# LayerNorm rows, y and late dO staged differently in the first part of a fused forward and backward block

## The chip, the core and the metric

The kernel runs on one core of one Trainium2 chip. The metric is the device time in microseconds (us); the time before is the median of five runs. The trace and the page that are quoted come from one profiled execution, whose own time stands in the table below.

## What is computed

A block of attention times a gate, forward and backward, for S = 2048 rows, D = 512, 32 heads of 16, and a hidden width F = 1792:

```python
xn = _layernorm(x)                       # eps 1e-5, no weights
s  = softmax(q k^T / 4) v  @ wo          # q, k, v = xn @ wqkv, 32 heads
y  = _layernorm(xn)                      # a second LayerNorm on the first
m  = gelu(y @ w1 + b1) @ w2 + b2
g  = silu(m)
out = x + s * g
```

The kernel returns `out` and the gradients with respect to x, wqkv, wo, w1, b1, w2 and b2 for a given grad_out. All tensors are bfloat16. The rows of x are cut into 16 tiles of 128 rows, and four tiles make a group.

## The kernel before

The program has three parts, one after the other, each written out by hand in the order of issue. Every engine takes its instructions in program order; a wait of one instruction holds all those behind it on its engine. DMAs are issued in order on SP (`nc.sync`), ACT (`nc.scalar`) or POOL (`nc.gpsimd`).

**First part, `phase_pre`.** It is the one that the change touches, apart from one line of the last part.

*k, v, q (L67 to L174).* x is loaded in four groups (L76, SP), wqkv and w1 by ACT (L78, L79). `ln1(g)` takes statistics of a group on DVE (`stats`: L86, L87, then a root on ACT, L89, a reciprocal and a product on DVE, L90, L91) and normalises: group 0 on DVE with transposes on PE (L96, L113, L114), the other groups on ACT (L102) with a DMA transpose on SP into xnT (L117). `ln2(g)` does the same once more on xn in place and sends it, transposed, to yT (L121 to L124). `hooks` says after which tile each is emitted. xn has three buffers for four groups, so that of group 0 is used again for group 3, after the transpose that reads it. For each tile PE makes k, v, q with 12 matmuls into three PSUM banks (L144, six banks in turn), ACT copies them (L149 to L151) into NSall (k and v; two buffers for four groups) and NQ, POOL squares k and q (L155, `sq`, three buffers), and DVE sums the squares by head (L130) one tile later. At the end of a group, SP stores NSall and NQ (L167, L168). After tile 5, SP issues the loads of b1, b2, w2 and the transposed wo (L160 to L163). Then the largest k norm is taken over all partitions on POOL (L174); `row_bound` uses it after h1(1).

*h1, m and gate (L182 to L304).* `h1(sc)` makes 14 matmul groups of four (L195) from yT and w1; DVE adds the bias into h1row (L198, eight buffers), ACT takes gelu (L199), SP stores h1row (L200). `m_step(t)` for each tile emits, in this order, a transpose of dso for tile t-2, `proj` for t-5 (dso times wo: L251, copy on ACT L253, store of NATQd_s on SP L255 after every fourth), `gate` for t-1 (DVE L218, L220, POOL L224 to L226; gB has four buffers), `slope_out` for t-3 (DVE L230, store of GB_s on SP L231) and the 14 matmuls of `m_mm` (L209). The order is h1(0), h1(1), the four tiles of group 0, h1(2), those of group 1, h1(3), and so on. The last four tiles of `proj`, from LATE = 12 on, use `late_sb`, which lies where w1 was and which attention will use as the third `eg` buffer. It holds a second copy of the transposed wo (L288, a DMA transpose on SP from DRAM), the late dsoT, and the late dO (`late_sb[:, 4:8]`). These steps are emitted by `rest` (L292) between the first steps of attention.

**Second part, `attention_core`.** 1024 steps for 16 pairs of heads, 16 steps to a block and 4 blocks to a pair. Each step has score matmuls (L786, L798) and exponentials on ACT (L812, L820), a product on DVE (L830) and accumulating matmuls; after every fourth step SP transposes what was made from `eg` to `tg` (L841). The three `eg` buffers change every four steps. Before a pair, POOL loads its operands from DRAM (L324 to L328), arranges them in `Pad`, and SP transposes them into KVT and QDT (L336, L345). For pair 0 the last 12 tiles of QDT come after the start: POOL's load of NATQd at step 7 (it reads NATQd_s), the arrangement at step 9, the transpose at step 11. Step 16 is the first to need them. The second set of KVT and QDT belongs to pair 1.

**Last part, `phase3`.** Weight and input gradients. `y_all` is computed again from xn_all on ACT (L545) between the matmuls of dw2.

Of the kernel before, what the change touches and what calls it, by code (L numbers as in the profile page):

```python
# [16 lines left out]
LATE = 12  # L17
# [20 lines left out]
def phase_pre(tc, k, A_x, A_wqkv, A_wo, B_w1, B_b1, B_w2, B_b2, grad_out):  # L38
# [4 lines left out]
    with ExitStack() as c1:  # L43
# [23 lines left out]
        with ExitStack() as c0:  # L67
# [3 lines left out]
            NSall = p0.tile([128, 2, NPAIR, 4, 2, NATW], bf16, name="NSall")  # L71
# [10 lines left out]
            def stats(g, src, rstd_all, nmr_all):  # L82
                s6 = wk0.tile([128, 4, nc.vector.BN_STATS_DIM], f32, name="ln_st")
                mv = wk0.tile([128, 4, nc.vector.BN_AGGR_DIM], f32, name="ln_mv")
                for i in range(4):
                    nc.vector.bn_stats(out=s6[:, i, :], in_=src[:, i, :])  # L86
                    nc.vector.bn_aggr(out=mv[:, i, :], in_=s6[:, i, :])  # L87
                rs = rstd_all[:, 4 * g:4 * g + 4]
                nc.scalar.activation(out=rs, in_=mv[:, :, 1], func=ACT.Sqrt, bias=k.eps_t[:], scale=1.0)  # L89
                nc.vector.reciprocal(out=rs, in_=rs)  # L90
                nc.vector.scalar_tensor_tensor(out=nmr_all[:, 4 * g:4 * g + 4], in0=mv[:, :, 0], scalar=-1.0, in1=rs, op0=ALU.mult, op1=ALU.mult)  # L91
                return mv, rs

            def norm(dst, src, mv, rs):
                for i in range(4):
                    nc.vector.tensor_scalar(out=dst[:, i, :], in0=src[:, i, :], scalar1=mv[:, i, 0:1], scalar2=rs[:, i:i + 1],  # L96
                                            op0=ALU.subtract, op1=ALU.mult)

            def norm_act(dst, src, g, rstd_all, nmr_all):
                for i in range(4):  # L100
                    t = 4 * g + i
                    nc.scalar.activation(out=dst[:, i, :], in_=src[:, i, :], func=ACT.Identity, bias=nmr_all[:, t:t + 1], scale=rstd_all[:, t:t + 1])  # L102

            def ln1(g):
                src = x_all[:, 4 * g:4 * g + 4, :]
                mv, rs = stats(g, src, k.rstd1, k.nmr1)
                xn[g] = p0.tile([128, 4, D], bf16, name="xn", bufs=3)
                if g == 0:
                    norm(xn[g], src, mv, rs)
                    for i in range(4):  # L110
# [4 lines left out]
                else:  # L115
                    norm_act(xn[g], src, g, k.rstd1, k.nmr1)
                    nc.sync.dma_start_transpose(out=xnT[:, 4 * g:4 * g + 4].rearrange("c t m q -> c (t m) q"),  # L117
                                                in_=xn[g][:].rearrange("q t c -> q (t c)"))

            def ln2(g):  # L120
                mv, rs = stats(g, xn[g], k.rstd2, k.nmr2)  # L121
                norm_act(xn[g], xn[g], g, k.rstd2, k.nmr2)
# [8 lines left out]
            ln1(0)  # L131
            ln1(1)
            hooks = {1: lambda: ln1(2), 3: lambda: ln2(0), 5: lambda: ln1(3), 8: lambda: ln2(1), 11: lambda: ln2(2), 14: lambda: ln2(3)}
            for t in range(NT):
# [3 lines left out]
                ns = NSall[:, i4 % 2]  # L138
# [14 lines left out]
                for dst, v in ((kn2, kk), (qn2, qq)):  # L153
                    sq = wk0.tile([128, H, DH], f32, name="sq", bufs=3)
                    nc.gpsimd.tensor_tensor(out=sq[:].rearrange("p (a j) c -> p a j c", j=2), in0=v, in1=v, op=ALU.mult)  # L155
                    sqs[t].append((dst, sq))
                if t in hooks:
                    hooks[t]()
                if t == 5:
# [4 lines left out]
                if t >= 1:  # L164
                    reduce_of(t - 1)
                if t % 4 == 3:
                    nc.sync.dma_start(out=k.NAT_s[:, :, t - 3:t + 1, :].rearrange("a p t c -> p a t c"), in_=ns.rearrange("p a t j c -> p a t (j c)"))  # L167
                    nc.sync.dma_start(out=k.NATQq_s[:, :, t - 3:t + 1, :].rearrange("a p t c -> p a t c"), in_=NQ[:].rearrange("p a t j c -> p a t (j c)"))  # L168
            reduce_of(NT - 1)
            nc.vector.tensor_copy(out=b1c[:], in_=b1_bf[:])  # L170
            nc.vector.tensor_copy(out=b2bc[:], in_=b2_bf[:])
            kmaxrun = wk0.tile([128, H], f32, name="kmaxrun", bufs=1)
# [9 lines left out]
        with ExitStack() as c0:  # L182
# [62 lines left out]
            def proj(t, pd=None):  # L245
# [6 lines left out]
                nd = ND[(t // 4) % 2] if t < LATE else late_sb[:, 4:8].rearrange("p b m q -> p (b m q)").rearrange("p (a b c) -> p a b c", a=NPAIR, b=4)  # L252
                nc.scalar.copy(out=nd[:, :, t % 4, :].rearrange("p a (j c) -> p a j c", j=2), in_=pd[:].rearrange("p (a j c) -> p a j c", a=NPAIR, j=2))  # L253
                if t % 4 == 3:
                    nc.sync.dma_start(out=k.NATQd_s[:, :, t - 3:t + 1, :].rearrange("a p t c -> p a t c"), in_=nd[:] if t < LATE else nd)  # L255
# [22 lines left out]
            for sc in range(4):  # L278
# [7 lines left out]
                if sc == 1:  # L286
                    late_sb = eg_as(2, [128, 16, IC, 128], "late_sb")
                    nc.sync.dma_start_transpose(out=late_sb[:, 0:4].rearrange("p b m q -> p b (m q)"), in_=A_wo)  # L288
            store_h(3)
            nc.scalar.activation(out=kmax2[:, 0:1], in_=k.eps_t[:], func=ACT.Exp)  # L290
# [5 lines left out]
            for t in range(NT - 5, LATE):  # L296
                proj(t)

            def rest(psum):
                proj(LATE, psum([128, 512], f32))  # L300
# [3 lines left out]
                for t in range(LATE + 1, NT):  # L304
                    proj(t, psum([128, 512], f32))
# [69 lines left out]
def phase3(ctx, tc, k, A_x, A_wqkv, A_wo, B_w1, B_w2, grad_out, out_0, out_1, out_2, out_3, out_4, out_5, out_6, out_7):  # L375
# [5 lines left out]
    with ExitStack() as c1:  # L381
# [23 lines left out]
        with ExitStack() as c2:  # L405
# [128 lines left out]
            for i in range(7):  # L534
# [8 lines left out]
                if i < 6:  # L543
                    for t in range(3 * i, min(3 * i + 3, NT)):
                        nc.scalar.activation(out=y_all[:, t, :], in_=xn_all[:, t, :], func=ACT.Identity, bias=k.nmr2[:, t:t + 1], scale=k.rstd2[:, t:t + 1])  # L545
# [121 lines left out]
def attention_core(ctx, tc, k, rest_of_pre, npairs=16, nqc=4):  # L667
# [330 lines left out]
    rest = rest_of_pre(lambda shape, dt: ps_z.tile(shape, dt, name="Z0", tag="z"))  # L998
# [56 lines left out]
def full_kernel(ctx, tc, A_x, A_wqkv, A_wo, B_x, B_w1, B_b1, B_w2, B_b2, grad_out,  # L1055
# [13 lines left out]
    k.nmr2 = persist.tile([128, NT], f32, name="nmr2")  # L1069
    k.ones_bf = persist.tile([128, 1], bf16, name="ones_bf")  # L1070
    nc.vector.memset(k.ones_bf[:], 1.0)
    persist.tile([128, 64], mybir.dt.uint8, name="pad_to_256")
# [90 lines left out]
```

## Time and profile before

| | |
|---|---|
| median of five runs | 2344.5 us (2332.8 to 2386.55) |
| the profiled execution: time | 2358.49 us |
| its span, first to last instruction | 2356.3 us |
| busy: PE, DVE, ACT, POOL | 2201.1, 1798.2, 1854.8, 1193.4 us |
| first part, up to the start of m (0 to 94.88 us): PE busy | 72.47 us |
| h1(2), h1(3), m and gate (94.88 to 188.09 us): PE busy | 88.78 us |
| start of attention (188.09 to 234.97 us): PE busy, mean clock | 38.74 us, 0.75 |
| rest of attention (234.97 to 1978 us): PE busy, mean clock | 1675.27 us, 0.95 |
| last part (1978 to 2356.3 us): PE busy | 325.84 us |

The page gives, for each engine, busy time and idle time, and for idle time what ended it. "A <- B: 7.4, 4, 2.3" in the list of waits says that A waited 7.4 us in total for B, in four places, 2.3 us in the longest. In the timeline a line is start, duration, engine (SPq, ACTq, POOLq are the queues that issue DMAs), source line, operation, output and inputs, and in brackets the idle time before it and what ended it. The clock is the share of full speed that TensorE was granted.

### The profile page before, as it was taken

How to read it: one execution, taken by the hardware profiler on the slowest of the kernel's cores; microseconds unless marked ns; L12 is line 12 of the kernel's file. 1: busy time of each engine (PE TensorE's matmuls, PEld its weight loads, DVE VectorE, ACT ScalarE, POOL GpSimd, SP SyncE). 2: the span in 40 equal slices, each digit the busy share in tenths (PEclk: the TensorE clock that was granted, in tenths of full speed). 3: DMA queues.
4: the chain of work that ended last, by engine and by line, in shares of the span. 5: the costliest groups of instructions: out<-in, count | busy, mean ns of one | idle time of the engine just before them, and what ended most of it. 6: DMA issues, size and time to landing. Idle time of an engine off the chain costs nothing.

```text
span 2356.3 us, 47583 instructions
## 1 busy us (share of the span) xinstructions
PE 2201.1 (93%) x18320; PEld 731.6 (31%) x18320; DVE 1798.2 (76%) x2994; ACT 1854.8 (79%) x2159; POOL 1193.4 (51%) x1956
## 2 busy tenths in 40 slices
PE   6998999999999999999999999999999998689997
PEld 3442222222222222222222222222222222234456
DVE  6766987898899799969987998988898893204641
ACT  6645988999999799979998999998998994221231
POOL 4355564656474647555665656574756554200020
PEclk9997997999999799969998999998998998999999
DMA  8778999999999999999999999999999998998546
GB/s 228 221 221 215 228 239 205 243 249 246 240 240 250 194 242 246 246 189 239 245 253 214 246 244 237 243 250 216 244 239 227 245 233 228 209 231 251 160 80 130
DMA packets 1763637, 530.42 MB, mean 225 GB/s; under 512 B 1684417, under 2 KB 1749074, under 8 KB 1763410
## 3 DMA queue, kind: packets, MB, share of 16 engines
q1 hardware_dynamic: 1719890, 468.25, 97.8%
q10 hardware_dynamic: 31200, 31.73, 4.7%
q0 software_dynamic: 12320, 27.41, 3.9%
q8 instruction: 143, 2.34, 0.4%
q14 instruction: 84, 0.69, 0.1%
HBM read 47.98 MB, written 58.33 MB: 45 GB/s over the span
## 4 chain that ended last, share of the span: by engine, by line
PE 50%; ACT 21%; DMA 12%; POOL 6%; issue 4%; DVE 2%; ACTq 0%; SPq 0%; POOLq 0%; DVEq 0%
ACT eg L812 9%; ACT e L820 9%; PE d L798 9%; PE s L786 8%; PE X L856 8%; DMA tg<-eg 7%; PE X L868 4%; PE Z L964 3%; PE X L880 2%; PE ps_dhg L581 2%; PE ps_dy L596 2%; PE ps_m L209 2%; DMA xt<-in_A_x_dram 1%; DMA hgc<-HGT_s 1%; PE ps_dw L539 1%
## 5 line engine op out<-in xcount | busy, mean ns | idle before, releaser
L830 DVE TENSOR_TENSOR eg<-d,eg 128x512 bf16<-128x512 f32 x2048 | 1349.7, 687 | 207.8 <-PE d L798 76.6
L812 ACT ACTIVATE eg<-s 128x1024 bf16<-128x1024 f32 x1024 | 1042.3, 1035 | 84.5 <-PE d L798 63.2
L798 PE MATMUL d<-QDT,KVT 32*128 32x512 bf16 x2048 | 816.6, 399 | 0.3 <-DVE eg L830 0.2
L820 ACT ACTIVATE e<-t 128x1024 bf16<-128x1024 f32 x640 | 663.6, 1037 | 53.6 <-PE t L772 52.2
L786 PE MATMUL s<-QDT,KVT 32*128 32x512 bf16 x2048 | 414.3, 399 | 47.2 <-ACT eg L812 41.8
L868 PE MATMUL X<-eg,NAT 128*32 128x512 bf16 x2048 | 419.3, 407 | 0.0
L856 PE MATMUL X<-eg,Lc 128*32 128x512 bf16 x2048 | 418.8, 406 | 0.0
L880 PE MATMUL X<-eg,NAT 128*17 128x512 bf16 x2048 | 412.4, 400 | 0.0
L798 PEld LDWEIGHTS <-KVT 32*128 32x128 bf16 x2048 | 186.4, 91 | 353.5 <-issue 353.4
L952 PE MATMUL Z<-e,W 128*32 128x512 bf16 x1280 | 261.5, 404 | 20.0 <-POOL W L919 19.0
L772 PE MATMUL t<-KVT,QDT 32*128 32x512 bf16 x1280 | 259.8, 400 | 1.8 <-ACT eg L812 1.5
L913 POOL TENSOR_TENSOR W<-NATQd,rL 128x128 bf16<-128x128 bf16 x64 | 25.8, 404 | 380.5 <-DVE rL L897 380.5
L964 PE MATMUL Z<-tg,W 128*32 128x512 bf16 x2048 | 213.0, 398 | 0.0
L786 PEld LDWEIGHTS <-KVT 32*128 32x128 bf16 x2048 | 116.9, 91 | 306.1 <-issue 304.4
L856 PEld LDWEIGHTS <-Lc 128*32 128x32 bf16 x2048 | 99.0, 93 | 288.8 <-issue 288.8
L952 PE MATMUL Z<-tg,W 128*32 128x512 bf16 x768 | 157.4, 407 | 0.0
L868 PEld LDWEIGHTS <-NAT 128*32 128x32 bf16 x2048 | 99.2, 94 | 170.5 <-issue 170.5
L719 POOL TENSOR_TENSOR bg_v<-bg_t 128x512 f32<-128x512 f32 x56 | 57.9, 1034 | 180.8 <-ACT bg_t L734 180.4
L978 DVE TENSOR_TENSOR acc<-Z,acc 128x512 f32<-128x512 f32 x192 | 130.5, 680 | 14.2 <-PE Z L964 14.2
L372 POOL TENSOR_TENSOR dx<-lnb_prod,lnb_dy 128x512 bf16<-128x512 f32 x16 | 20.9, 1311 | 233.6 <-DMA dout<-in_grad_out_dram 210.1
L952 PEld LDWEIGHTS <-W 128*32 128x32 bf16 x2048 | 109.2, 93 | 48.7 <-POOL W L919 23.3
L880 PEld LDWEIGHTS <-NAT 128*17 128x17 bf16 x2048 | 93.0, 88 | 61.4 <-issue 61.4
(173 smaller groups left out, 2760.6 us busy)
## 6 DMA issues: line engine op xcount, KB each, us to landing
H1T_s<-h1row SPq DMA_DIRECT2D x56, 128.0 KB, 1.8
HGT_s<-hgT SPq DMA_DIRECT2D x4, 1792.0 KB, 7.8
bg_x<-H1T_s POOLq DMA_DIRECT2D x56, 128.0 KB, 5.3
GP_s<-bg_m POOLq DMA_DIRECT2D x56, 128.0 KB, 5.4
gp<-GP_s ACTq DMA_DIRECT2D x8, 896.0 KB, 6.9
DH1T_s<-dh1T SPq DMA_DIRECT2D x4, 1792.0 KB, 9.6
NAT_s<-NSall SPq DMA_DIRECT2D x4, 1056.0 KB, 6.4
NAT<-NAT_s POOLq DMA_DIRECT2D x16, 264.0 KB, 5.8
```

Of the source, the lines that this page charges most:

```text
L772: nc.tensor.matmul(t[:, hj, :], lhsT=op["QDT"][r:r + 32, q0:q0 + 128], rhs=op["KVT"][r:r + 32, kc * 512:(kc + 1) * 512], start=True, stop= ...
L786: nc.tensor.matmul(s[:, hj, :], lhsT=op["KVT"][r:r + 32, kb * 128:(kb + 1) * 128], rhs=op["QDT"][r:r + 32, qc * 512:(qc + 1) * 512], start ...
L798: nc.tensor.matmul(d[:], lhsT=op["KVT"][r:r + 32, kb * 128:(kb + 1) * 128], rhs=op["QDT"][r:r + 32, qc * 512:(qc + 1) * 512], start=True, ...
L812: nc.scalar.activation(out=cur["eg"][1][:, :, kb % 4, :, :].rearrange("k b h q -> k h b q"), in_=st_s.pop(g)[:].rearrange("k h (b q) -> k ...
L820: nc.scalar.activation(out=e[:], in_=st_t.pop(g)[:], func=ACT.Exp)
L830: nc.vector.tensor_tensor(out=gts[:, kb % 4, hj, :].rearrange("k (b q) -> k b q", b=4), in0=ds[hj][:].rearrange("k (b q) -> k b q", b=4), ...
L856: nc.tensor.matmul(X[64 + 32 * hj:96 + 32 * hj, :], lhsT=Lc[:], rhs=et[:, :, kb % 4, hj, :], start=(kb == 0), stop=False, skip_group_check ...
L868: nc.tensor.matmul(X[32 * hj:32 * hj + 32, :], lhsT=NATt[:, kb, hj, 1:33], rhs=et[:, :, kb % 4, hj, :], start=(kb == 0), stop=(kb == 15), ...
L880: nc.tensor.matmul(X[64 + 32 * hj:64 + 32 * hj + 17, :], lhsT=NATt[:, kb, hj, 0:17], rhs=gts[:, kb % 4, hj, :], start=False, stop=(kb == 1 ...
L952: nc.tensor.matmul(Z[32 * hj:32 * hj + 32, :], lhsT=blk[j]["W1"][:, qb, hj, :], rhs=ev[:, hj], start=(i == 0), stop=False, tile_position=( ...
L964: nc.tensor.matmul(Z[c:c + 32, :], lhsT=blk[j]["W2"][:, qb, hj, :], rhs=gv[:, :, hj, qb, :], start=(i == 1), stop=(i >= 2), tile_position= ...
L978: nc.vector.tensor_tensor(out=av, in0=Z[:], in1=av, op=ALU.add)
```

## The change

- Statistics and rows are two functions. `ln_stats` takes DVE statistics of x. `ln_rows` forms rstd1 and nmr1, and from the first variance also the variance of xn (variance times rstd1 squared), from which `ln_apply` makes rstd2 with a root and a reciprocal. There is no second set of statistics, and the mean of xn is taken as zero.
- `ln_apply` normalises and transposes as `ln1` did. y is xn times rstd2: group 0 on DVE after tile 5, groups 1 to 3 on POOL after the loop.
- The schedule: rows of group 1 and statistics of group 2 after tile 0, group 1 is normalised after tile 1, and so on as `hooks` says.
- NSall has three buffers, sq has five, and the sums of squares are taken two tiles later.
- b1, b2, w2 and the transposed wo are issued after tile 0.
- The second copy of wo is made by DVE from the first.
- Late dO is staged in the second operand set's QDT, and its store is issued by ACT.
- The small Exp that loads the table of exponentials is emitted after the last `proj` before attention.
- y_all in the last part has no bias; nmr2 is gone and the padding keeps the size.

```diff
-            NSall = p0.tile([128, 2, NPAIR, 4, 2, NATW], bf16, name="NSall")
+            NSall = p0.tile([128, 3, NPAIR, 4, 2, NATW], bf16, name="NSall")
...
+            def ln_stats(g):
                 s6 = wk0.tile([128, 4, nc.vector.BN_STATS_DIM], f32, name="ln_st")
+                mvs[g] = wk0.tile([128, 4, nc.vector.BN_AGGR_DIM], f32, name="ln_mv")
                 for i in range(4):
+                    nc.vector.bn_stats(out=s6[:, i, :], in_=x_all[:, 4 * g + i, :])
+                    nc.vector.bn_aggr(out=mvs[g][:, i, :], in_=s6[:, i, :])
+
+            def ln_rows(g):
+                mv = mvs.pop(g)
+                rs, rs2, nm = (t_[:, 4 * g:4 * g + 4] for t_ in (k.rstd1, k.rstd2, k.nmr1))
                 nc.scalar.activation(out=rs, in_=mv[:, :, 1], func=ACT.Sqrt, bias=k.eps_t[:], scale=1.0)
                 nc.vector.reciprocal(out=rs, in_=rs)
+                nc.vector.scalar_tensor_tensor(out=nm, in0=mv[:, :, 0], scalar=-1.0, in1=rs, op0=ALU.mult, op1=ALU.mult)
+                nc.vector.tensor_tensor(out=rs2, in0=mv[:, :, 1], in1=rs, op=ALU.mult)
+                nc.vector.tensor_tensor(out=rs2, in0=rs2, in1=rs, op=ALU.mult)
+                if g == 0:
+                    ln_apply(g, mv)
+
+            def ln_apply(g, mv=None):
+                rs, rs2, nm = (t_[:, 4 * g:4 * g + 4] for t_ in (k.rstd1, k.rstd2, k.nmr1))
+                xn[g] = p0.tile([128, 4, D], bf16, name="xn", bufs=3)
                 for i in range(4):
                     t = 4 * g + i
+                    if g == 0:
+                        nc.vector.tensor_scalar(out=xn[g][:, i, :], in0=x_all[:, t, :], scalar1=mv[:, i, 0:1], scalar2=rs[:, i:i + 1],
+                                                op0=ALU.subtract, op1=ALU.mult)
                         pt = psT.tile([128, IC, 128], bf16, name="tp_ps", tag="tp")
                         for b in range(IC):
                             nc.tensor.transpose(pt[:, b, :], xn[g][:, i, b * 128:(b + 1) * 128], k.ident_bf[:])
                         nc.scalar.copy(out=xnT[:, i, :, :], in_=pt[:])
+                    else:
+                        nc.scalar.activation(out=xn[g][:, i, :], in_=x_all[:, t, :], func=ACT.Identity, bias=nm[:, i:i + 1], scale=rs[:, i:i + 1])
+                if g > 0:
                     nc.sync.dma_start_transpose(out=xnT[:, 4 * g:4 * g + 4].rearrange("c t m q -> c (t m) q"),
                                                 in_=xn[g][:].rearrange("q t c -> q (t c)"))
+                nc.scalar.activation(out=rs2, in_=rs2, func=ACT.Sqrt, bias=k.eps_t[:], scale=1.0)
+                nc.vector.reciprocal(out=rs2, in_=rs2)
 
             def ln2(g):
-                mv, rs = stats(g, xn[g], k.rstd2, k.nmr2)
-                norm_act(xn[g], xn[g], g, k.rstd2, k.nmr2)
+                for i in range(4):
+                    rs2 = k.rstd2[:, 4 * g + i:4 * g + i + 1]
+                    (nc.vector if g == 0 else nc.gpsimd).tensor_scalar(out=xn[g][:, i, :], in0=xn[g][:, i, :], scalar1=rs2, scalar2=None, op0=ALU.mult)
                 nc.sync.dma_start_transpose(out=yT[:, 4 * g:4 * g + 4].rearrange("c t m q -> c (t m) q"),
                                             in_=xn[g][:].rearrange("q t c -> q (t c)"))
...
-            ln1(0)
-            ln1(1)
-            hooks = {1: lambda: ln1(2), 3: lambda: ln2(0), 5: lambda: ln1(3), 8: lambda: ln2(1), 11: lambda: ln2(2), 14: lambda: ln2(3)}
+            ln_stats(0)
+            ln_rows(0)
+            ln_stats(1)
+            hooks = {0: [(ln_rows, 1), (ln_stats, 2)], 1: [(ln_apply, 1)], 2: [(ln_rows, 2), (ln_stats, 3)], 3: [(ln_apply, 2)],
+                     5: [(ln2, 0), (ln_rows, 3)], 6: [(ln_apply, 3)]}
...
-                    sq = wk0.tile([128, H, DH], f32, name="sq", bufs=3)
+                    sq = wk0.tile([128, H, DH], f32, name="sq", bufs=5)
...
-                if t == 5:
+                if t == 0:
                     nc.sync.dma_start(out=b1_bf[:], in_=B_b1.rearrange("(c p) -> p c", p=128))
                     nc.sync.dma_start(out=b2_bf[:], in_=B_b2.rearrange("(o d) -> o d", o=1).to_broadcast([128, D]))
                     nc.sync.dma_start(out=w2_sb[:], in_=B_w2.rearrange("(c p) d -> p c d", p=128))
                     nc.sync.dma_start_transpose(out=woT[:], in_=A_wo)
-                if t >= 1:
-                    reduce_of(t - 1)
+                if t >= 2:
+                    reduce_of(t - 2)
...
+            reduce_of(NT - 2)
             reduce_of(NT - 1)
             nc.vector.tensor_copy(out=b1c[:], in_=b1_bf[:])
             nc.vector.tensor_copy(out=b2bc[:], in_=b2_bf[:])
+            for g in range(1, 4):
+                ln2(g)
...
-            def proj(t, pd=None):
+            def proj(t, pd=None, nd_late=None):
...
-                nd = ND[(t // 4) % 2] if t < LATE else late_sb[:, 4:8].rearrange("p b m q -> p (b m q)").rearrange("p (a b c) -> p a b c", a=NPAIR, b=4)
+                nd = ND[(t // 4) % 2] if t < LATE else nd_late.rearrange("p (a b c) -> p a b c", a=NPAIR, b=4)
...
-                    nc.sync.dma_start(out=k.NATQd_s[:, :, t - 3:t + 1, :].rearrange("a p t c -> p a t c"), in_=nd[:] if t < LATE else nd)
+                    (nc.sync if t < LATE else nc.scalar).dma_start(out=k.NATQd_s[:, :, t - 3:t + 1, :].rearrange("a p t c -> p a t c"), in_=nd[:] if t < LATE else nd)
...
-                    nc.sync.dma_start_transpose(out=late_sb[:, 0:4].rearrange("p b m q -> p b (m q)"), in_=A_wo)
+                    nc.vector.tensor_copy(out=late_sb[:, 0:4].rearrange("p b m q -> p b (m q)"), in_=woT[:])
             store_h(3)
-            nc.scalar.activation(out=kmax2[:, 0:1], in_=k.eps_t[:], func=ACT.Exp)
...
             for t in range(NT - 5, LATE):
                 proj(t)
+            nc.scalar.activation(out=kmax2[:, 0:1], in_=k.eps_t[:], func=ACT.Exp)
...
-                        nc.scalar.activation(out=y_all[:, t, :], in_=xn_all[:, t, :], func=ACT.Identity, bias=k.nmr2[:, t:t + 1], scale=k.rstd2[:, t:t + 1])
+                        nc.scalar.activation(out=y_all[:, t, :], in_=xn_all[:, t, :], func=ACT.Copy, scale=k.rstd2[:, t:t + 1])
...
-    rest = rest_of_pre(lambda shape, dt: ps_z.tile(shape, dt, name="Z0", tag="z"))
+    rest = rest_of_pre(lambda shape, dt: ps_z.tile(shape, dt, name="Z0", tag="z"), OP[1]["QDT"][:])
```

## The prediction

> **What bounds the kernel now.** I read the totals, then clock and busy time in stretches of 10 us, then waits, chain and timeline up to 260 us. PE is busy for 93% of the span and carries the middle, so only PE time lost or gained counts. The edits lie before 235 us, one apart, and there PE stands idle in a few places. The waits from 0 to 260 us (total, times, longest, us):
>
> ```profile
> PE pk L144 <- ACT NSall L149: 7.4, 4, 2.3
> ...
> DVE gB L218 <- DMA GB_s<-gB: 6.4, 2, 5.3
> ...
> ACT eg L812 <- DMA NATQd_s<-late_sb: 6.1, 1, 6.1
> ...
> PE s L786 <- ACT eg L812: 5.3, 4, 4.7
> ...
> PE ps_h L195 <- ACT NSall L149: 2.3, 1, 2.3
> ...
> PE ps_h L195 <- DVE h1row L198: 2.1, 1, 2.1
> ```
>
> Three places: k/v/q and its border to h1 (lines 1, 5, 6), one gate step (line 2), the start of attention (lines 3, 4). How the first arises, in the timeline of all engines:
>
> ```profile
> 44.53 0.18 DVE L87 BATCH_NORM_AGGREGATE ln_mv<-ln_st 128x2 f32<-128x6 f32 x1
> 44.75 0.30 ACT L89 ACTIVATE rstd<-ln_mv,eps_t 128x4 f32<-128x4 f32 x1 [2.14 <-DVE ln_mv L87]
> ...
> 45.49 2.92 ACT L102 ACTIVATE xn<-xn,nmr,rstd 128x512 bf16<-128x512 bf16 x4 [0.44 <-DVE nmr L91]
> ...
> 48.95 1.02 PE L144 MATMUL pk<-wqkv_sb,xnT 128*128 128x512 bf16 x4 [2.29 <-ACT NSall L149]
> ```
>
> ACT waits for statistics, then normalises; 5.7 us pass without a PSUM copy, and PE with six banks (0.862 us each) idles 2.3 us. The other two are SP's. Its queue:
>
> ```profile
> 149.51 0.39 SPq L203 DMA_DIRECT2D HGT_s<-hgT  x1
> 149.99 7.15 SPq L288 DMA_TRANSPOSE late_sb<-in_A_wo_dram  x1
> ...
> 159.13 0.41 SPq L231 DMA_DIRECT2D GB_s<-gB  x1
> ...
> 201.59 4.99 SPq L841 DMA_TRANSPOSE tg<-eg  x1
> 206.67 0.53 SPq L255 DMA_DIRECT2D NATQd_s<-late_sb  x1
> ```
>
> One transpose holds SP 7.15 us and GB_s with it; another holds the late dO store, whose buffer is that of eg number 8. What follows (us; PE, PEld, DVE, ACT, POOL busy; clock; DMA share; GB/s):
>
> ```profile
> 160.00:170.00 10.00, 6.18 (x20) 2.37 (x19) 4.72 (x7) 1.59 (x3) 6.94 (x8) 0.68 0.75 237
> ...
> 210.00:220.00 10.00, 7.60 (x34) 1.35 (x33) 5.44 (x8) 5.42 (x6) 5.34 (x9) 0.57 1.03 200
> 220.00:230.00 10.00, 10.00 (x52) 1.96 (x49) 6.42 (x10) 5.27 (x6) 4.43 (x7) 0.50 0.93 211
> ```
>
> After each gap PE runs at half clock.
>
> **The Trainium skill.** (1) "TensorE: Matmul & The Clock Gate", Part 1: an idle window of about 3.4 us halves the clock, about 3.4 us of work restore it. The trace agrees at 164 us (4.3 us idle, then 0.50 until about 171), not at 213 us, where 0.50 lasts some 20 us of full work; the waits of 2.3 us leave 1.00. (2) "DMA: Bandwidth & Descriptors", Queues, rings and completion order: SP and ACT each own a row of rings, and an engine alternates between rows. The profile has q1 with SP's bytes and q10 with ACT's 3.41 MB. (3) "SBUF — State Buffer", Who interferes with whom: a VectorE operation with two SBUF inputs contends with GpSimd, one with a single SBUF input does not. L224 took 0.85 beside such an operation and 0.63 alone; h1row reads PSUM, so y on POOL should run undisturbed.
>
> **First part (edits to LN, y, staging, weights).** Removed: 16 second statistics on DVE (0.67+0.18 each, 3.2 us a group) and 16 second normalisations on ACT (2.93 a group). ACT falls from 12 copies at a pitch of 0.48 + 2×2.93 + 2×0.3 = 12.3 us a group of four tiles to 9.3; PE needs 48×0.2155 = 10.35, so PE becomes the bound. New small rows (two 128x4 products, a second root, a reciprocal) delay the start by 0.2.
>
> *Tile 4.* xn[1] used to be normalised before tile 0's copies; now after tile 1's, which end at 20.6. +2.93 = 23.5, +4.1 (median landing of xnT) = 27.6; PE is through tile 3 at 25.1+0.2: 2.3 us idle. SP is the other gate: b1, b2, w2, woT now stand ahead of this transpose. x_all, wqkv, w1, b2 and w2 are 7.5 MB at the 400 GB/s seen from 6 to 16 us, 18.7 us from 2 us on, plus 1.5 for b1's tiny pieces: SP leaves woT (9.15 before, until w2 had landed) near 22, before 23.5. Take no more; if 3 us late, PE idles 5 us.
>
> *Tile 9.* xn[3] takes xn[0]'s buffer, so ACT waits for yT[0]. SP: xnT[2] to 31.6, NAT_s and NATQq (0.65+2.27) to 34.5, yT[0] issued near 35.1, landed 3.8 later at 38.9; ACT is there at 36.0, resumes at 42.1. PE has done its six banks at 40.6 and restarts at about 42.6: 2.0. Behind that ACT wait stand only copies.
>
> PE ends k/v/q at T = 27.6+0.2+12×2.588+2.0 = 60.9 (before 64.2, and then 5 more idle).
>
> *Border to h1.* y of groups 1 to 3 is twelve POOL tensor_scalars after the last square (T+1.8). The trace has none with a column scalar; rows of the shape: 0.62 (L718), 0.85 (L224 disturbed), ceiling 1.04 (a two-input product, L155). I take 0.62: 7.4, done T+9.2. SP must issue all three yT (last until T+11) before the first H1T store, and that lands 1.9 later, T+13.5 with queueing. h1row has eight buffers: DVE begins at T+4.1, fills eight by T+9.7, waits; PE fills six banks to T+12.1, restarts at T+14.2: 2.1 lost. Then stores (0.71 apart) keep up with PE (0.862). kmax (partition reduction) now follows y on POOL, near T+13; row_bound needs it at about T+26: hidden. h1(0)+h1(1) are 112×0.2155 = 24.1. End: 60.9+24.1+2.1 = 87.1 against 94.9 before: **−7.8**. The third staging tile and five sq buffers take away no wait that I find in the trace: 0.
>
> **Copy of A_wo.** L288 goes; DVE copies 128x2048 bf16 instead. No such row: 0.69 by the table of "VectorE: DVE Perf Modes" (The perf-mode tier table), at most 4×0.405 = 1.6 by L96. It stands after h1(3)'s last row, where DVE idles 1.21 and then 2.05: hidden, else 0.4. PE starts of ps_m: 157.44, 166.75, 172.70; without the stall two periods of 4.11 from 157.44 give 165.7: **−7.0**. After h1(2) the same order without a transpose cost DVE 1.07 us and PE next to nothing, so what is late next (HGT_s's 1.8 MB ahead of GB_s) is no bound.
>
> **Late dO.** Staged in QDT of the second operand set, written next near step 40, and lying where w2_sb was, which PE last reads at 188; no new wait. Its store goes to ACT after the copy that ends at 201.75, ahead of the SP transpose that held it; 0.5 of issue delays exp(5). exp(8) no longer waits: 205.4 (204.07+1.3) instead of 211.21. At full clock DVE paces block 0, 2×0.687 = 1.37: exp(15) at 215.0. exp(16) needs QDT's tail: store landed 201.8+4.4 = 206.2, POOL's load +5.8 = 212.0, Pad copy 212.6, SP free of the second tg at 206.8+7.8 = 214.6, landed +3.2 = 217.8, exp(16) at 218.2. Before 226.63: −8.4. Three more steps took 7.84 at half clock; at the mean step of 1.73 (1743 us over 1009 steps) 5.2: −2.6. With the 0.5: **−10.5**. Moving the Exp table load (1.28) behind two ACT copies frees PE's bank earlier but leaves exp(0) where it is: 0. In the last part, y loses its bias (0.80 each, under ps_dw of PE): 0.
>
> Sum 7.8+7.0+10.5 = 25.3. The profiled execution (span 2356.3 in 2358.5) would give 2333.2. It is 14 us above the median of the runs, about one half-clock stretch of attention more; the three places come from the order of the program, so I set the sum against the median: 2344.5−25.3 = 2319.2.
>
> **Rivals.** *A, POOL's y gates h1.* At 1.04 each y ends at T+14.3, H1T lands at T+18.1, PE loses 6.7 instead of 2.1 and about 2 of half clock: sum 18.7, 2325.8. For: in-order SP; against: 0.62 for the same shape.
> *B, a new wait at exp(16).* The 2.8 us for QDT's tail (215.0 to 217.8) sit just under the gap that halves the clock. A stretch costs: 207 matmuls in 33 us (345 to 378, 0.50) against 286 in 30 (380 to 410), 33−21.7 = 11.3. Sum 14.0, 2330.5.
> *C, slower: more half-clock stretches in attention.* Six were seen after 235 us, several just after PE had waited 1.4 to 3.3 us for POOL's W at a pair border. An earlier start moves where these gaps fall. From three more (33.9 > 25.3) it is slower, 2353; from five more over 1%. Against: attention's order is unchanged, so none is expected.
> *D, the change does not free GB_s*: HGT_s ahead of it holds the gate step as long; sum 18.3, 2326. Against: the 1.07 after h1(2).
> *E, none of the three PE gaps in the first part*: 6.4 more, 2312.8.
>
> **How the numbers follow.** Forecast 0.45 (own range 2311 to 2327), A 0.15, B 0.15, C 0.1, D 0.05, E 0.1. One per cent (about what a measurement can tell from no change) is 23.4 us, below the forecast by only 1.9: six tenths of the forecast's share, E and a little of A, B, D give 0.45 faster; C spread beyond 1% with unseen trouble 0.08. Range: 2302 (E and more) to 2341 (B with a loss elsewhere), leaving out C and a tail below.
>
> **What would show it.** PE's waits for NSall gone but for about 2 us each at tiles 4 and 9; last pq near 61, first ps_m near 87. SP without a 7 us transpose near 142, clock 1.00 there. exp(8) waiting for no DMA, clock 1.00 in block 0, a wait for QDT of 2 to 3 us at step 16. Wrong if SP still sits in woT after 24 us, if y's twelve take over 10 us, or if half-clock stretches in attention differ by more than one from before.

## The result and the profile after

The kernel after takes 2355.91 us (median of 43 runs, 2327.98 to 2391.85) beside 2347.26 for the kernel before (80 runs, 2321.66 to 2392.85): a ratio of 1.003, 95% interval 1.001 to 1.005. No gain, where I had forecast 25 us and a range that ended at 2341. Ratios leave out runs over 1.5% above the fastest of their kernel; means and clocks below are of all runs, so the two need not agree (h4_before_filler has a ratio of 0.997 and a mean 7.6 us over before's).

Where the profiled executions part (us; span of before 2356.3, of after 2365.6). T is the start of the last matmul of k, v, q, ps_m is the PSUM tile of m, and exp(n) is the start of the exponential of step n of attention:

| | before | after | change | forecast |
|---|---|---|---|---|
| k/v/q ends (T) | 64.2 | 65.2 | +1.0 | −3.3 |
| T to the first ps_m | 30.7 | 39.6 | +8.9 | −4.5 |
| first ps_m to exp(0) | 97.1 | 90.7 | −6.4 | −7.0 |
| exp(0) to exp(19) | 42.5 | 42.1 | −0.3 | −10.5 |
| exp(19) to exp(64) | 73.4 | 78.3 | +4.9 | 0 |
| exp(64), sum | 307.9 | 316.0 | +8.1 | −25.3 |

After exp(64) the difference goes with attention's stretches at half clock (1.5 us at step 100, 10.2 at the end of attention), and the last part takes 377.4 in place of 378.3. Of the forecast steps, one came as forecast: from the first ps_m to exp(0). The waits from 0 to 250 us, in the same list as was read before the change:

```profile
DVE h1row L206 <- DMA H1T_s<-h1row: 15.6, 1, 15.6
...
PE ps_h L203 <- DVE h1row L206: 13.4, 1, 13.4
...
POOL NATQd L332 <- DMA tg<-eg: 11.2, 1, 11.2
...
PE s L794 <- DMA QDT<-Pad: 6.3, 1, 6.3
...
PE pk L149 <- DMA xnT<-xn: 4.0, 1, 4.0
...
PE pk L149 <- ACT NSall L154: 2.0, 1, 2.0
```

The waits for GB_s (6.4) and for the late store at exp(8) (6.1) are gone, and so are most of those for NSall (7.4). In their place stand a wait of PE for h1row, one for QDT, and one for xnT. The first, in the timeline of all engines:

```profile
67.31 18.55 POOL L125 TENSOR_SCALAR xn<-xn,rstd 128x512 bf16<-128x512 bf16 x12
...
69.31 5.35 DVE L206 TENSOR_SCALAR h1row<-ps_h,b1c 128x512 bf16<-128x512 f32 x8
...
73.58 13.90 SPq L126 DMA_TRANSPOSE yT<-xn  x3
87.58 7.03 SPq L208 DMA_DIRECT2D H1T_s<-h1row  x14
90.22 10.39 DVE L206 TENSOR_SCALAR h1row<-ps_h,b1c 128x512 bf16<-128x512 f32 x14 [15.56 <-DMA H1T_s<-h1row]
...
91.02 9.17 PE L203 MATMUL ps_h<-yT,w_sb 128*128 128x512 bf16 x34 [13.36 <-DVE h1row L206]
```

POOL takes 18.55 us for the twelve y operations. SP, in order, waits for each of the three y before it issues the first H1T store; DVE fills its eight h1row buffers and waits for that store; PE fills its banks and waits for DVE. The chain is the one forecast, with twelve operations of 1.55 us in place of 0.62. No neighbour slows them: DVE stands idle from 74.7 us on, and the operations after that take 1.56 us like those before.

Tile 4, and SP ahead of it (start, duration):

```profile
6.62 7.94 SPq L166 DMA_DIRECT2D b_bf<-in_B_b_dram  x1
...
15.99 7.87 SPq L168 DMA_TRANSPOSE woT<-in_A_wo_dram  x1
...
23.98 6.84 SPq L117 DMA_TRANSPOSE xnT<-xn  x2
...
28.78 1.14 PE L149 MATMUL pk<-wqkv_sb,xnT 128*128 128x512 bf16 x4 [4.01 <-DMA xnT<-xn]
...
29.72 1.91 PE L149 MATMUL pv<-wqkv_sb,xnT 128*128 128x512 bf16 x4
```

The weight loads hold SP until 23.9, and the four matmuls of pv take 1.91 where they take 1.03 at full clock: the gap was followed by half clock. The late dO (timeline, then the list of DMA issues, whose last column is the time from issue to landing):

```profile
207.66 13.55 SPq L849 DMA_TRANSPOSE tg<-eg  x2
...
208.91 0.38 ACTq L263 DMA_DIRECT2D NATQd_s<-QDT  x1
...
218.16 0.58 POOL L332 DMA_DIRECT2D NATQd<-NATQd_s  x1 [11.18 <-DMA tg<-eg]
```

```profile
NATQd_s<-QDT ACTq DMA_DIRECT2D x1, 512.0 KB, 8.7
```

The store lands at 208.9 + 8.7 = 217.6, and POOL's load, which reads what it writes, goes out at 218.16; the profile names a tg transpose, which landed about then, as the one that came last. The forecast had this store ahead of the first tg transpose; it was issued 1.25 us behind it. Step 16 waits 6.3 us for QDT. In stretches of 10 us (columns as in the prediction):

```profile
80.00:90.00 10.00, 0.00 (x0) 0.00 (x0) 0.00 (x0) 0.00 (x0) 5.86 (x4) 0.54 0.57 143
...
160.00:170.00 10.00, 10.00 (x54) 4.66 (x52) 5.56 (x8) 5.04 (x9) 7.31 (x8) 1.00 0.99 322
...
230.00:240.00 10.00, 9.70 (x54) 2.40 (x50) 6.29 (x11) 7.39 (x9) 4.58 (x14) 0.50 1.19 222
```

At the border to h1 all engines but POOL stand still; the gate stretch, which had 6.18 us of PE work at 0.68, is full at 1.00; after the QDT wait the clock is at half.

### The profile page after: what moved, and what is told of

The parts are those of the page before. It is cut to its first block, busy times and chain, and to the rows that moved or that the text cites. A ratio compares the mean times of both kernels' runs of the same rounds, so it can differ in the third digit from the quotient of the medians.

```text
span 2365.6 us, 47546 instructions
## 1 busy us (share of the span) xinstructions
PE 2200.5 (93%) x18320; PEld 730.8 (31%) x18320; DVE 1788.6 (76%) x2971; ACT 1844.8 (78%) x2143; POOL 1212.7 (51%) x1968
## 4 chain that ended last, share of the span: by engine, by line
PE 47%; ACT 21%; DMA 14%; POOL 6%; issue 4%; DVE 2%; ACTq 0%; POOLq 0%; SPq 0%; DVEq 0%
ACT e L828 9%; ACT eg L820 9%; PE d L806 9%; DMA tg<-eg 8%; PE s L794 8%; PE X L864 8%; PE X L876 4%; PE Z L972 3%; PE X L888 2%; PE ps_dy L604 2%; PE ps_dhg L589 2%; PE ps_m L217 2%; DMA xt<-in_A_x_dram 1%; DMA hgc<-HGT_s 1%; PE ps_dw L547 1%
```

## The experiments

Every run has its mean granted clock beside its time. Over 576 runs of all kernels the time falls by 16.2 us for 0.01 of mean clock, with 3.6 us of scatter left. At half clock half of the clock is missing, so 0.01 of 2356 us stands for 47 us at half clock. By this slope a microsecond at half clock costs 0.34 and a stretch of 33 us costs 11.3, the price that the prediction took from one stretch. "Equal clock" below is the difference of the mean times from before less this part: 0.6 to 1.4 us uncertain within a session (runs of some kernels and of before on one chip), some 2 between sessions. It also takes away the half clock that a kernel's own waits bring, so it is no full account of a change. ± is one standard error.

The events are of one execution each, and they scatter. In the six traces with y on VectorE whose first part is the same program (e1, g4, f3, f4, h2, h3), the first ps_m comes at 89.1 to 94.9, because T does: 62.1 to 66.2. Steadier is the border, from T to the first ps_m: 29.1 to 30.8 us in the four traces with before's first part, 39.1 and 39.6 with POOL's y as changed (f2, after), 27.0 to 28.7 with y on VectorE, 28.5 with the sends moved (e2), 29.2 and 29.3 with two operations (h1, g1), 24.4 with both (g2, g3).

| kernel | ratio to before, 95% | mean clock less before's | equal clock, us | first ps_m | exp(0) | exp(19) | exp(64) |
|---|---|---|---|---|---|---|---|
| before | 1 | | | 94.9 | 192.0 | 234.5 | 307.9 |
| after | 1.003 [1.001, 1.005] | (1) | −2.2 | 104.8 | 195.5 | 237.7 | 316.0 |
| e1_y_dve | 0.989 [0.986, 0.992] | +0.0065 ± 0.0020 | −10.3 | 94.5 | 185.2 | 226.0 | 301.5 |
| g4_y_dve_again | 0.994 [0.991, 0.997] | +0.0015 ± 0.0026 | −10.5 | 94.9 | 185.8 | 226.2 | 302.9 |
| e2_stores_first | 0.996 [0.992, 1.000] | +0.0020 ± 0.0020 | −3.7 | 91.5 | 186.0 | 225.6 | 299.5 |
| f2_pool_const | 1.009 [1.005, 1.014] | −0.0063 ± 0.0030 | +1.1 | 104.7 | 195.4 | 231.4 | 308.1 |
| g1_two_op | 1.005 [1.003, 1.008] | −0.0059 ± 0.0019 | −7.2 | 94.8 | 185.5 | 225.2 | 304.6 |
| h1_two_op_again | 1.006 [1.002, 1.010] | −0.0063 ± 0.0025 | −6.2 | 95.0 | 185.6 | 227.5 | 302.7 |
| g2_two_op_first | 0.992 [0.988, 0.995] | +0.0026 ± 0.0020 | −8.0 | 90.1 | 183.1 | 222.7 | 295.5 |
| f1_dve_loads5 | 0.992 [0.986, 0.997] | +0.0022 ± 0.0028 | −8.9 | 92.1 | 182.8 | 220.9 | 294.9 |
| g3_all | 0.994 [0.990, 0.997] | +0.0028 ± 0.0021 | −8.2 | 88.3 | 180.9 | 222.8 | 301.0 |
| e3_wo_copy | 1.000 [0.997, 1.002] | −0.0007 ± 0.0018 | −2.2 | 93.0 | 183.6 | 226.9 | 305.2 |
| e4_late_do | 1.000 [0.996, 1.003] | −0.0005 ± 0.0030 | −1.6 | 93.0 | 187.3 | 227.9 | 300.9 |
| f4_dve_no_late | 0.997 [0.994, 1.000] | −0.0028 ± 0.0022 | −7.6 | 89.7 | 180.4 | 225.7 | 304.4 |
| f3_dve_store_sp | 1.003 [1.000, 1.006] | −0.0075 ± 0.0019 | −8.9 | 94.5 | 185.2 | 221.8 | 308.5 |
| h3_dve_store_pool | 0.993 [0.989, 0.997] | +0.0030 ± 0.0026 | −8.1 | 93.6 | 184.3 | 223.6 | 301.9 |
| h2_dve_filler | 0.998 [0.993, 1.002] | +0.0040 ± 0.0024 | −7.9 | 89.1 | 181.4 | 218.9 | 305.9 |
| h4_before_filler | 0.997 [0.992, 1.001] | −0.0045 ± 0.0026 | +0.2 | 94.7 | 193.2 | 235.4 | 310.5 |

(1) 0.9497 over 44 runs, before 0.9508 over 240 of the other sessions. For the session of the result, before's clock is not on record; its mean time of 2348.7 us points to 0.955, an estimate by the slope above.

**Is it POOL's y, and does SP's order make it a stall?** Two edits of the changed kernel; in the second, y stays on POOL, and its transposes of groups 2 and 3 leave ln2 for send_y:

```diff
# e1_y_dve, g4_y_dve_again
-(nc.vector if g == 0 else nc.gpsimd).tensor_scalar(
+nc.vector.tensor_scalar(
# e2_stores_first
             h1(0)
+            send_y(2)
+            send_y(3)
```

e1_y_dve: 

> The changed kernel with y of groups 1 to 3 on VectorE instead of POOL, all else kept. Theory: the border to h1 is lost because POOL's multiplication by a column takes 1.56 us (12 of them 18.6 us) and SP stands in the three y transposes behind it, so that H1T stores begin 20 us late; with VectorE (12 x 0.34 us) the first ps_m matmul starts near 93 us instead of 104.8, and the time falls by 10 to 15 us against the changed kernel, to 4 to 8 us below the kernel before. Rival: the loss is in the early weight loads and the late xnT, before the border; then the first ps_m stays above 102 us and the time within 3 us of the changed kernel.

e2_stores_first: 

> The changed kernel with y still on POOL, but the transposes of y of groups 2 and 3 issued on SP after the stores of h1(0) instead of ahead of them. Theory (it is the order on SP that turns POOL's slowness into a stall): h1row never waits long for a store, first ps_m near 91 us, time as with y on VectorE. Rival (POOL's 18.6 us bind h1 by themselves, through y or the partition maximum): first ps_m at 98 us or later, less than half of the gain.

g4_y_dve_again: 

> The changed kernel with y of groups 1 to 3 on VectorE, once more. It had 0.989 of before, 23 us, although its profiled execution was only 6 us ahead of before at step 64 of attention. If the rest is a property of the kernel: again 0.987 to 0.992. If it came from how attention's stretches at half clock happened to fall on that chip: nearer to 0.997, the 6 us.

Both bring the first ps_m back, from 104.8 to 94.5 and to 91.5, and the border from 39.6 to 28.7 and 28.5, so both halves of the chain are shown. In the second POOL still needs 18.55 us, and nothing waits for it for long, because SP has sent the stores (its queue):

```profile
71.40 1.65 SPq L130 DMA_TRANSPOSE yT<-xn  x1
73.15 7.06 SPq L212 DMA_DIRECT2D H1T_s<-h1row  x14
...
80.30 5.04 SPq L130 DMA_TRANSPOSE yT<-xn  x2
```

On VectorE the twelve take 3.24 us together. Of the 21 us that e1 gained in the mean, half goes with the clock: the repeat has 13, and the same 10 at equal clock.

**Why is POOL slow?** First the operand, then the form:

```diff
# f2_pool_const (y of groups 1 to 3 isn't scaled by rstd2)
-scalar1=rs2, scalar2=None, op0=ALU.mult)
+scalar1=rs2 if g == 0 else 1.0, scalar2=None, op0=ALU.mult)
# g1_two_op, h1_two_op_again
-scalar1=rs2, scalar2=None, op0=ALU.mult)
+scalar1=rs2, scalar2=0.0, op0=ALU.mult, op1=ALU.add)
```

f2_pool_const: 

> The changed kernel, y of groups 1 to 3 on POOL, but multiplied by the constant 1.0 instead of the column rstd2 (that multiplication is left out, so y there is xn). Theory: the column operand is what makes a POOL tensor_scalar take 1.56 us; with a constant it takes 0.62 as in the rows that the prediction used, 12 take 7.4 us, h1 waits about 2 us for its first stores and the first ps_m starts near 91 us. Rival: it is the bf16 in-place operation or this place in the program, and it stays near 1.5 us, first ps_m near 104.

g1_two_op: 

> The changed kernel; the twelve y operations of groups 1 to 3 stay on POOL but are written with two operations (times the column, then plus 0.0), as the line of bg_m and the line of q1 are, in place of one. Theory (POOL is slow in the form with one operation): 0.62 to 0.85 us each, 7.4 to 10 us for the twelve in place of 18.6, so that the premise of my forecast holds; the last yT is issued near 78 in place of 87, the wait of h1row for its store falls from 15.6 to under 6 us, first ps_m at 92 to 96 in place of 104.8; the time 0.5 to 1.2% below before. Rival (POOL needs about 1.5 us for this shape whatever the form, when something else runs beside it or the data come from this place): 1.4 to 1.6 us each, first ps_m near 104.8, ratio 1.00.

h1_two_op_again: 

> The changed kernel with y on POOL in two operations, once more. Every run has its mean granted clock beside its time. Over all runs so far the time falls by 16.2 us for 0.01 of mean clock, and 3.5 us of scatter remain; at equal clock this kernel was 7 us ahead of before, but its mean clock was 0.9444 against 0.9503, which cost 9.5 us and made it 0.5% slower. If the lower clock belongs to this kernel: again 0.943 to 0.947, ratio 1.003 to 1.008. If it is chance of that session: clock 0.949 to 0.953, ratio 0.995 to 0.999. At equal clock 6 to 8 us ahead either way.

The groups of y on POOL (busy us, mean ns), of after, f2_pool_const and g1_two_op:

```profile
L125 POOL TENSOR_SCALAR xn<-xn,rstd 128x512 bf16<-128x512 bf16 x12 | 18.6, 1567 | 0.0
```

```profile
L125 POOL TENSOR_SCALAR xn<-xn 128x512 bf16<-128x512 bf16 x12 | 17.6, 1499 | 0.0
```

```profile
L125 POOL TENSOR_SCALAR xn<-xn,rstd 128x512 bf16<-128x512 bf16 x12 | 8.3, 708 | 0.0
```

My theory of the column operand fell: a constant is nearly as slow. With a second operation that adds zero, the same work takes 0.71 us in place of 1.57. The first ps_m comes at 94.8, 10 us earlier, and 4 to 5 us show at equal clock. PE still waits 3.1 us for h1row, and the half clock behind that wait costs 1.9. Yet this kernel is the slower one by its ratio, on two chips: its mean clock is 0.006 lower both times. Its start of attention is within 0.3 us of that of y on VectorE, whose clock is higher. As far as two sessions tell, the clock thus belongs to the kernel and not to the session; what sets it I can't name.

**The rest of the first part.** The sends moved as in e2_stores_first together with the two operations; then also the loads back after tile 5 (`if t == 0` becomes `if t == 5`), which f1_dve_loads5 does with y on VectorE:

f1_dve_loads5: 

> y on VectorE, and b1, b2, w2 and wo loaded after tile 5 again, as before the change. Theory: loaded after tile 0 they hold SP (until 24 us) and the DMA engines when xnT of group 1 is due, and PE waits 3.3 to 4.3 us at tile 4; loaded later, the wait at tile 4 falls to about 2 us (xn of group 1 is itself made late), the first ps_m starts 2 to 4 us earlier than with y on VectorE alone (94.5), time 2 to 4 us less. Rival: the loads then hold SP when the transposes of xnT of group 3 and y of group 0 are due, ACT waits longer at tile 6 and nothing is won. A second question: y on VectorE alone came out 23 us below the kernel before, though its trace is only 8.5 us ahead at step 19 of attention; if that is y's place itself, this kernel is 20 us or more below too, if it was chance, some 10.

g2_two_op_first: 

> The run before this one, with yT of groups 2 and 3 also sent after the stores of h1(0). Theory: the two cures act on the same stall, so they don't add: against the version that only moves the sends (first ps_m 91.5) at most 2 us earlier, 89 to 92, and no wait of h1row for its store over 2 us. If POOL's slow form is not cured by two operations, 91.5 as with the sends alone. Time 0.4 to 1.2% below before. Rival (something else than y and its sends holds h1): first ps_m over 95.

g3_all: 

> The run before this one, with the loads of b1, b2, w2 and the transposed A_wo issued after tile 5, as in the kernel before. Theory: PE's wait at tile 4 falls from 4.3 to about 2 us, first ps_m 2 us earlier again (87 to 90, as near to the forecast's 87.1 as anything gets), exp(0) near 180; time 1.0 to 1.5% below before, unless attention adds stretches at half clock. Rival (a stall at tile 9 or at the border takes the place of that of tile 4): first ps_m as in the run before.

With two operations and the sends moved, PE waits nowhere at the border, which takes 24.4 us where 26.2 were forecast. With the loads moved too, the wait at tile 4 falls to 2.1 us, tile 9 keeps one of 4.4 to 4.5, and the first ps_m comes at 88.3 (the forecast was 87.1). T is then 63.4 and 63.9, within the 62.1 to 66.2 of the kernels with early loads, so what the loads alone are worth isn't shown. At equal clock no more than 9 us come of all this.

**The other two steps alone, and the late dO undone.** e3_wo_copy and e4_late_do are the kernel before with one step; f4_dve_no_late is y on VectorE with the late dO as before.

```diff
# e3_wo_copy
-nc.sync.dma_start_transpose(out=late_sb[:, 0:4].rearrange("p b m q -> p b (m q)"), in_=A_wo)
+nc.vector.tensor_copy(out=late_sb[:, 0:4].rearrange("p b m q -> p b (m q)"), in_=woT[:])
# e4_late_do (f4_dve_no_late: the reverse): all lines of the diff that bear on nd_late, such as
-nd = ND[(t // 4) % 2] if t < LATE else late_sb[:, 4:8].rearrange("p b m q -> p (b m q)").rearrange("p (a b c) -> p a b c", a=NPAIR, b=4)
+nd = ND[(t // 4) % 2] if t < LATE else nd_late.rearrange("p (a b c) -> p a b c", a=NPAIR, b=4)
```

e3_wo_copy: 

> The kernel before with one edit: the second copy of wo made by VectorE instead of a DMA transpose on SP. Prediction: PE's stall of 4.3 us at 160 us and the half clock after it go, 7.0 us less than before (0.997). Rival: the stores of GB_s stay behind HGT_s's 1.8 MB and the stall stays: no change.

e4_late_do: 

> The kernel before with one edit: late dO staged in the second operand set's QDT and stored by ACT. Prediction: 10.5 us less (0.9955), with exp 8 waiting for nothing, exp 19 of attention 32 us after exp 0 instead of 42.5. Rival, from the trace after: the store now shares the DMA engines with the first tg transpose and lands in 8 to 9 us, so the wait only moves to QDT at step 16: exp 19 some 39 to 42 us after exp 0, gain of 0 to 4 us.

f4_dve_no_late: 

> y on VectorE, late dO staged and stored as before the change (in late_sb, by SP). Theory (the late dO edit only moves a wait from exp 8 to step 16): exp 19 some 42 us after exp 0 against 40.8 with the edit, time within 3 us of y on VectorE alone. Rival (the edit is worth the forecast 10.5 us): 8 us or more above it.

The copy shortens the run of ps_m by 6.7 us (92.8 to 86.1), but exp(64) comes only 2.6 us earlier: after exp(19) 4.9 are given back at half clock (203 to 244 us). The late dO alone takes 1.9 off exp(0) to exp(19). One pair of traces says little here: in the four without this step (before, e3, f4, h4) that stretch takes 42.1 to 45.3 us, mean 43.3, and in the twelve that have it as changed (f3 and h3, below, alter it) 36.0 to 42.1, mean 39.9. That is 3.4 us of the 10.5. Undone under y on VectorE it costs some 2.7 at equal clock, of two sessions. Neither step is resolved in its ratio.

**The store's landing.**

```diff
# f3_dve_store_sp: y on VectorE, store on SP, the first tg one step later
-(nc.sync if t < LATE else nc.scalar).dma_start(
+nc.sync.dma_start(
...
+        if g == 4:
+            emit_dmat(3)
...
-        emit_dmat(g)
+        if g != 3:
+            emit_dmat(g)
# h3_dve_store_pool: y on VectorE
-(nc.sync if t < LATE else nc.scalar).dma_start(
+(nc.sync if t < LATE else nc.gpsimd).dma_start(
```

f3_dve_store_sp: 

> y on VectorE, and the late dO store back on SP, with the first tg transpose held until after it (one step later). Theory: the store on ACT shares the DMA engines with that transpose and lands in 8.6 us instead of 4.4, and the chain store, POOL load, Pad, QDT transpose is what step 16 waits for (5.0 us); on SP ahead of the transpose it lands in 4.4, the wait for QDT at step 16 falls to 0 to 2 us, exp 19 comes 3 to 5 us sooner after exp 0 (40.8 with the store on ACT). Rival: tg arrives later, exp 12 waits for it, and the gain is eaten.

h3_dve_store_pool: 

> y on VectorE, and the late dO store issued by POOL in place of ACT. My prediction had it land 4.4 us after its issue; on ACT beside the tg transposes it took 8.7, on SP ahead of them 3.3. If the transposes hold the DMA engines themselves, it lands after 8 us or more here too, and step 16 waits as before (1 to 6 us for QDT). If it was ACT's ring that gave way to SP's: 4 to 5 us, POOL's load of NATQd 3 to 4 us earlier, no wait at step 16, exp(19) minus exp(0) near 38 in place of 40.6. Time 0.988 to 0.994.

From issue to landing, f3, h3 and f2_pool_const:

```profile
NATQd_s<-QDT SPq DMA_DIRECT2D x1, 512.0 KB, 3.3
```

```profile
NATQd_s<-QDT POOLq DMA_DIRECT2D x1, 512.0 KB, 11.4
```

```profile
NATQd_s<-QDT ACTq DMA_DIRECT2D x1, 512.0 KB, 4.5
```

Ahead of the tg transposes the store lands in 3.3 us from SP, and in 4.5 from ACT in f2_pool_const, where it happened to be issued 0.12 us before the first of them. Behind the first it takes 8.6 to 9.6 from ACT (ten traces) and 11.4 from POOL. So it isn't ACT's ring that gives way: the place before or behind the transposes decides. What they hold isn't shown. In f2_pool_const exp(0) to exp(19) takes 36.0 us, the shortest of all. In f3_dve_store_sp landing early did not pay. With tg(0) a step later the buffer of eg waits (f3's timeline):

```profile
206.50 2.85 ACT L820 ACTIVATE eg<-s 128x1024 bf16<-128x1024 f32 x3 [2.85 <-DMA tg<-eg]
```

exp(19) comes 4.2 us earlier than in e1_y_dve, the clock is then at half from 208 to 262 us, and exp(64) comes 7 later. At equal clock this kernel isn't ahead of y on VectorE alone (−8.9, beside −10.3 and −10.5).

**Does the place where attention starts decide?** Sixteen matmuls that nobody reads, ahead of step 0:

```diff
+    fl = ps_z.tile([128, 512], f32, name="Z0", tag="z")
+    for _ in range(16):
+        nc.tensor.matmul(fl[:].rearrange("p (o q) -> p o q", o=4), lhsT=k.ident_bf[:],
+                         rhs=k.ident_bf[:].rearrange("p (o q) -> p o q", o=1).to_broadcast([128, 4, 128]), start=True, stop=True)
     emit_s(0)
```

h2_dve_filler: 

> y on VectorE, and 16 more matmuls (128x512, 0.2155 us each at full clock, read by nobody) on PE ahead of the first step of attention: a later start of at most 3.4 us with a busy PE. Rival C of my prediction (where attention starts decides how many stretches at half clock it meets): the mean clock moves by more than 0.004 from that of the kernel without them (0.9518 and 0.9579). Theory (the stretches depend on gaps inside attention, which don't change): clock within 0.951 to 0.958, and the time 0 to 3.4 us over that of y on VectorE.

h4_before_filler: 

> The kernel before, with the 16 extra matmuls of the run with y on VectorE ahead of attention. Rival C: mean clock off by more than 0.004 from that of before (0.9507 over 185 runs). Theory: clock 0.948 to 0.953, time 0 to 3.4 us over before, ratio 1.000 to 1.002.

With y on VectorE the clock stays among those of its other two runs. Before's falls by 0.0045 ± 0.0026, which is over the 0.004 that was named but no proof. And h2's first part ended 5 us earlier than theirs by itself (its PE didn't wait at tile 9), so that attention started earlier and not later. Rival C is neither shown nor excluded.

## Why the prediction was wrong

**The step that failed first: "I take 0.62: 7.4, done T+9.2", with "ceiling 1.04".** The twelve took 18.6 us and y was done at T+20.7. The three rows that I bounded it by all came from other forms, two with two operations and one with two inputs, and the operation here has one: it lay outside both ends (and f2_pool_const shows that the column has little part in it). The chain behind it was right. PE lost 13.4 in place of 2.1, and with some 2 us at half clock after that the border took 39.6 where 26.2 was forecast. This was rival A, with 1.55 us where A had 1.04, and at twice its price (13.4 us over the forecast, where A had 6.6); the list of what would prove me wrong named it ("y's twelve take over 10 us"). With the premise mended (g1_two_op: twelve operations of 0.71 us) the border takes 29.3: even then the forecast was 3 us short, about 2 of it half clock after the wait.

**T, 65.2 for 60.9.** Tile 4 began at 28.8 for 27.8: SP left woT at 23.9, where I had said "near 22", and xnT landed later. Tile 9 waited 2.0, as forecast, but that was luck: in the eight other traces with the same program up to there it waits 1.6 to 5.1 us six times and not at all twice. The four operations of y of group 0 on VectorE take 0.35 us each, but 1.12 where they start while POOL squares. Where this befell one of the four, tile 9 waited 2.0 us or less; where it befell three, 2.7 to 5.1. The forecast has no such term. The rest is "the waits of 2.3 us leave 1.00". That did not hold in the trace before either: after the wait of 2.1 us for h1row the clock is at half from 74.8 to 78.2. Here half clock followed both waits, and the next twelve matmuls took 4.3 and the next sixteen 5.1 us where 2.59 and 3.45 were due: 1.7 each. 60.9 + 1.0 + 1.7 + 1.7 = 65.3. So the new LN order doesn't bring T forward (62.1 to 66.2, before 63.9 to 64.1); with y cured it shortens the border by 1 to 2 us, and with two operations and the sends moved by 5 to 6.

**A_wo, −7.0: right** (−6.4 in after, −6.7 alone), and no bound stood behind it. The copy takes 0.68 us, where I had 0.69. Rival D fell.

**Late dO, −10.5: −0.3 in this pair of traces, 3.4 over all.** exp(8) waits for no DMA, as forecast. But from exp(0) to exp(8) it took 17.3 us in place of the 13.4 that I had: PE stood 1.1 and 1.7 us around the table load and ran at half clock from 197 to 207. That put the store's issue 13.4 us after exp(0) for 10 in the sum, and behind the first tg transpose, where I had it ahead. The term "store landed 201.8+4.4" was the one most wrong: ahead of the transpose 4.5 is right (f2_pool_const), behind it the store takes 8.7. Load and QDT followed, and step 16 waited 6.3 us for 2.8.

**Half clock after it: rival B,** to which I gave 0.15. It ran from 224 to 255 us, and exp(19) to exp(64) took 4.9 us more than before. But every kernel here, before too, has 10 us or more of half clock between 200 and 265 us, whichever wait stands there, and exp(19) to exp(64) takes 76.4 us in the mean of the four traces without the late dO step and 76.7 with it. That the step costs anything there isn't shown.

**In sum:** y and its sends cost 8 us at equal clock (e1_y_dve against after), and the other steps together won 10 of 25. After's −2.2 at equal clock is then undone by clock: over all sessions its mean clock is 0.001 below before's, in its own session more. I had argued rival C down because attention's order is unchanged. The order is unchanged in every kernel here, and the mean clock still differs by up to 0.015, which is 24 us. When a gap of PE is followed by half clock can be read from the traces (last section); what sets the mean clock of a kernel stays open. So does why POOL's form with one operation is slow. Faster than both kernels of the case, by about one per cent, are y on VectorE (0.989 and 0.994) and two operations with the sends moved (0.992).

## What to carry to other kernels

Price an operation from a row of its own form, engine and operand count; where none exists, the nearest row is no ceiling, and an engine that takes over work in front of an in-order queue should be tried by itself first. A transfer's landing time holds only for the traffic it was measured in. Take the mean granted clock with every run: at equal clock a few microseconds could be told apart here, where plain medians of the same kernel lay 10 us apart. One trace of a program is one draw: before an event is put down to an edit, compare it over all traces that share the program up to there.

## What the runs showed of the hardware

- POOL's tensor_scalar, 128x512 bf16: 1.57 us with one operation and a column, 1.50 with one operation and a constant, 0.71 with two operations.
- The Trainium skill, "TensorE: Matmul & The Clock Gate", Part 1, puts the idle window that halves the clock at about 3.4 us and calls it free-running. The traces agree with the second: in each, the clock changes only on a grid of 3.413 us, which lies elsewhere from execution to execution (in after half clock begins at 29.58, 46.64, 80.78 and 196.83 us: 5, 10 and 34 steps apart). They don't need a whole idle window. From 15 to 188 us, over 18 traces, half clock followed all 34 grid cells of full clock in which PE was busy for less than 40%, 11 of the 29 with 40 to 55%, and none of the 788 with more. So 2.01 us idle within one cell brought half clock (after, tile 9), and 3.26 us across two did not (e1_y_dve, tile 4). The same wait of 2.48 us at the border, with y on VectorE, was followed by half clock in five traces and not in two. In the first part one cell of nearly full work mostly ended it (38 of 40 over 93%); in attention, after 235 us, half clock went on after 686 of 844 such cells (over 97%), and why stays open.
- VectorE's tensor_scalar, 128x512 bf16 with one input in SBUF: 0.35 us, but 1.12 where it starts while POOL squares.
- A 512 KB store landed 3.3 us (SP) or 4.5 us (ACT) after its issue when it went ahead of the tg transposes, and 8.6 to 9.6 (ACT) or 11.4 (POOL) behind the first.
- Holding SP: 7.94 us for the load of b2 spread over 128 partitions (it stands behind that of b1), 7.87 for the transposed A_wo from DRAM.
